# Block-causal attention with a ReGLU feed-forward on Trainium2: last-key scores placed behind the first score visit, and visits and products shifted, in the third tile

## The chip, the core and the metric

The kernel runs on one core of one Trainium2 chip, as one program. The metric is device time in microseconds (us). All engines work side by side: TensorE (PE) multiplies matrices, ScalarE (ACT) does exponentials and ReLU, VectorE (DVE) does elementwise arithmetic, GpSimd (POOL) issues the casting loads and does some elementwise work, SyncE (SP) issues the transposing transfers. Each engine executes its own list of instructions in the order in which the program wrote them; they meet at semaphores.

## The reference: what is computed

There are 8 batches, 8 heads, 576 positions, head size 64. Attention is causal by blocks of 64: a query sees the keys of its own block and of all earlier blocks. The attention output, joined over the heads to rows of 512, goes through a feed-forward with gate and value.

```python
scores = scale * np.matmul(q, k.transpose(0, 1, 3, 2))
scores = np.where(block_i >= block_j, scores, -1000000000.0)
attn = softmax(scores)                       # over the keys
x = np.matmul(attn, v)                       # to (8 * 576) x 512
out = (np.maximum(x @ w_gate, 0.0) * (x @ w_val)) @ w_out    # 512 -> 1536 -> 512
```

## The kernel before, in words

**Feed-forward tiles.** The rows of a batch are cut into 512 main rows and 64 tail rows. The feed-forward works on nine tiles of 512 rows: tile j (0 to 7) is the main rows of batch j, tile 8 collects the tail rows of all batches. One tile has 12 columns f of the hidden layer. For each f, four TensorE matmuls make the gate (over c = 0 to 3, a quarter of the 512 inputs each) and four make the value (L862, `ffn_gen`). ScalarE takes the ReLU of the gate (`relu`, L872), VectorE multiplies it with the value into `hT` (`hidden`, L882). From the third tile on (j >= 2) the product with `w_out` is done by a seven-product scheme (`seven_products`, L785), for which VectorE makes sums of `hT` (L744, one step after each ReLU from f = 4 on).

**Attention beside it.** The attention of batch b runs inside the feed-forward tile of batch b - 1, so in the third tile (j = 2) TensorE also works on the fourth batch (b = 3). It goes by rounds r = 4b + head pair, so here r = 12 to 15, each with these steps, named by a letter and r:

- s: the score visit (`visit`, L428, matmuls L451). It makes all scores of a head pair in four PSUM areas: the single buffer `one`, one `ffnp` buffer, and two `sc` buffers. From batch 3 on it also holds the 64 tail queries (`qTt`), which come right after the first pair of matmuls. ScalarE then takes the exponentials: one of `one`, one of `ffnp` (L463), one of the first `sc` buffer (L456).
- e: the exponential of the second `sc` buffer (L456), on ScalarE alone.
- c: zeroing of corners in the exponentials, on VectorE here (L1017), on POOL for r = 15.
- a, b: the product of the exponentials with v for the first and the second head (`products_with_v`, L586 and L600, 15 matmuls), then a normalisation on VectorE (L523, L525, L532).
- x: a transposing transfer of the result to `xT`, issued by SP (`to_xT_dma`, L635).

Two more steps belong to a batch: L3 is `last_keys(3)` (L469): four matmuls (L473) of the transposed last keys `kTt` with `qTt` into `one`, and an exponential into `attnL` (L480), which the products a and b read. B2 is the tail product of the third batch (`tail_av`, L539, matmuls L548).

**Where operands come from.** `d3` (at place 260.7) issues four transposing transfers from SP: `qTm`, `kTm` (L348), then `qTt`, `kTt` (`tails_by_dma`, L116 to L120). `l4`, `lv4` are POOL's loads of the fifth batch, `d4` its four transposes.

**Buffers.** PSUM holds two `sc` buffers, one `one` and three `ffnp` buffers (L47 to L55). Gates, values, the second head's part of a visit, and for r = 12, 13, 14 also both products a and b (`HOW`, L1367 to L1369) share the three `ffnp` buffers; a new user waits until the readers of the old one are done. `a15`, `b15` use `sc`.

**The order** is written out by hand. The dictionary `AT` gives every step a place. A place counts feed-forward matmuls: 144 to a tile, the third tile begins at 288. From the third tile on the first 96 places of a tile are its 96 gate and value matmuls. The loop emits the feed-forward up to a step's place and then the step, in order of places; steps with equal places keep the order of the dictionary:

```python
for n in sorted(acts, key=lambda n: AT[n]):
    at = int(place_of(AT[n]))
    ffn(at - place[0])
    place[0] = max(place[0], at)
    acts[n]()
```

Below, "place 28" means 28 matmuls into the third tile (316 in `AT`). Later tiles use one fixed pattern (`STEADY`, L1397): visits at places 2, 30, 58 and 86, then e 6, c 13, a 20 and b 24 places after their visit, the last products later.

Of the kernel before, what the change touches and what calls it, by code (L numbers as in the profile page):

```python
# [17 lines left out]
def kernel(  # L18
# [1003 lines left out]
    with tc.manual_schedule(engines={E.PE, E.DVE, E.Activation, E.Pool, E.SP}):  # L1022
# [82 lines left out]
        def mains_1(hp):  # L1105
# [209 lines left out]
            "E2": 283.05,  # L1315
            "L2": 286.35,
            "A2": 299.9,
            "s12": 316,
            "L3": 315.45,
            "l4": 319.56,  # L1320
            "e12": 324,
            "B2": 326.23,
            "lv4": 333.84,
            "c12": 331,
            "a12": 337,
            "b12": 341,
            "s13": 335,
            "e13": 343,
            "x12": 341.1,
            "d4": 356.12,  # L1330
            "c13": 350,
            "s14": 354,
            "e14": 362,
            "c14": 369,
            "a13": 356,
            "b13": 360,
            "x13": 360.1,
            "a14": 375,
            "b14": 379,
            "s15": 373,  # L1340
            "e15": 381,
            "x14": 379.1,
            "c15": 388,
            "a15": 400,
            "b15": 404,
# [210 lines left out]
```

## Time and profile before

| | us |
|---|---|
| median of 3 runs | 360.32 |
| fastest and slowest of them | 359.3, 362.04 |
| the profiled execution, its own time | 360.77 |
| its span, first to last instruction | 358.9 |
| TensorE busy in the span | 346.0 (96%) |
| VectorE busy | 208.3 (58%) |
| ScalarE busy | 180.5 (50%) |
| POOL busy | 141.1 (39%) |

The mean granted TensorE clock over the span was 0.997. The span is what the profile's views cover; the execution's own time is 1.87 us longer. The views name instructions by line, engine, operation and tile; `x4` means that four were merged into one row; the time given for a merged row is from the start of the first to the end of the last. The times of one matmul overlap with the next: a 128x512 matmul is shown as 379 ns, and four in a row start about 0.865 us before the row that follows them, or 0.216 us each. A number in square brackets is idle time of the engine before the row, and what ended it.

### The profile page before, as it was taken

The page shows a single profiled execution, that of the slowest core. Times are in us where ns is not written, and L with a number is a line of the kernel's source. Part 1 is how long each engine was busy: PE and PEld are TensorE (multiplying, and loading weights), DVE is VectorE, ACT ScalarE, POOL GpSimd, SP SyncE. Part 2 cuts the span into 40 slices and gives each one's busy share as a digit, 9 for nine tenths or more (in the row PEclk, how much of TensorE's full clock was granted, in tenths as well). Part 3 has the DMA queues.
Part 4 walks back from the last instruction along what each step waited for, and adds up shares of the span by engine and source line. Part 5 has one row for each costly group of instructions (what it writes and reads, how often), then busy time and mean ns, then how long its engine had stood idle before and what let it go on. Part 6 is the DMA issues. An engine that isn't in the chain of part 4 may idle for free.

```text
span 358.9 us, 8064 instructions
## 1 busy us (share of the span) xinstructions
PE 346.0 (96%) x3173; PEld 202.1 (56%) x3173; DVE 208.3 (58%) x522; ACT 180.5 (50%) x286; POOL 141.1 (39%) x183
## 2 busy tenths in 40 slices
PE   6899999999997999999999999999999999999994
PEld 2544455545543448555865576557755684485473
DVE  4663445678454775576637772667366745644661
ACT  5933766686335662556355545655475513322321
POOL 4647645599918602591049302950200020020002
PEclk9999999999999999999999999999999999999998
DMA  8999989999999993699549963998310030003004
GB/s 242 297 355 372 328 210 288 195 141 167 183 179 129 132 148 82 138 147 134 93 134 136 120 127 116 131 137 141 112 46 15 17 111 29 2 14 105 1 0 119
DMA packets 155495, 50.02 MB, mean 139 GB/s; under 512 B 134465, under 2 KB 151873, under 8 KB 155457
## 3 DMA queue, kind: packets, MB, share of 16 engines
q0 software_dynamic: 70480, 8.85, 48.4%
q1 hardware_dynamic: 76432, 31.47, 43.2%
q10 hardware_dynamic: 8544, 9.18, 7.8%
q8 instruction: 25, 0.41, 0.5%
q14 instruction: 14, 0.11, 0.1%
HBM read 37.75 MB, written 9.44 MB: 131 GB/s over the span
## 4 chain that ended last, share of the span: by engine, by line
PE 87%; DMA 6%; ACT 3%; POOL 1%; DVE 1%; issue 1%; SPq 0%; DVEq 0%; POOLq 0%
PE ffnp L862 50%; PE ffnp L785 13%; PE one L785 5%; PE ffnp L957 3%; PE sc L451 3%; PE ffnp L586 2%; PE one L451 2%; DMA xT<-xnat 2%; DMA stage<-in_moe_w_gate_dram 2%; PE one L586 1%; DMA stage<-in_k_dram 1%; PE one L862 1%; ACT attnT L456 1%; PE ffnp L548 1%; PE sc L586 1%; ACT attnT L463 1%
## 5 line engine op out<-in xcount | busy, mean ns | idle before, releaser
L882 DVE TENSOR_TENSOR hT<-gate_sb,ffnp 128x512 bf16<-128x512 bf16 x106 | 72.6, 685 | 73.7 <-PE ffnp L862 49.0
L862 PE MATMUL ffnp<-xT,wv 128*128 128x512 bf16 x376 | 102.0, 379 | 0.0
L872 ACT ACTIVATE gate_sb<-ffnp 128x512 bf16<-128x512 f32 x103 | 62.1, 605 | 78.3 <-PE ffnp L862 77.1
L862 PE MATMUL ffnp<-xT,wg 128*128 128x512 bf16 x364 | 100.3, 379 | 0.6 <-DVE xT L630 0.3
L862 PEld LDWEIGHTS <-wv 128*128 128x128 bf16 x432 | 39.8, 98 | 45.3 <-issue 3.6
L829 POOL TENSOR_TENSOR ob<-ob 128x512 f32<-128x512 f32 x7 | 8.8, 1263 | 142.6 <-ACT ob L826 142.6
L862 PEld LDWEIGHTS <-wg 128*128 128x128 bf16 x432 | 39.9, 98 | 43.2 <-issue 3.0
L456 ACT ACTIVATE attnT<-sc 128x1024 bf16<-128x1024 f32 x56 | 57.5, 1042 | 0.0
L785 PEld LDWEIGHTS <-stage 128*128 128x128 bf16 x420 | 40.3, 98 | 6.2
L744 DVE TENSOR_TENSOR stage<-hT 128x512 bf16<-128x512 bf16 (+2 forms) x84 | 38.5, 485 | 0.9
L586 PEld LDWEIGHTS <-attnT 128*128 128x128 bf16 x640 | 26.5, 98 | 13.4 <-issue 2.2
L785 PE MATMUL ffnp<-stage 128*128 128x256 bf16 x252 | 31.4, 273 | 0.0
L463 ACT ACTIVATE attnT<-one 128x512 bf16<-128x512 f32 (+1 forms) x28 | 15.0, 536 | 25.9 <-PE ffnp L451 25.8
L339 POOL DMA_DIRECT2D q_bf<-in_q_dram x20 | 18.0, 913 | 23.4 <-DVE hT L882 18.0
L339 POOL DMA_DIRECT2D v_bf<-in_v_dram x30 | 24.1, 842 | 0.9 <-PE sc L451 0.4
L957 PE MATMUL ffnp<-wo,hT 128*128 128x512 bf16 x96 | 23.6, 379 | 0.0
L451 PEld LDWEIGHTS <-kTm 64*128 64x128 bf16 x384 | 13.3, 94 | 14.1 <-issue 8.1
L451 PE MATMUL sc<-qTm,kTm 64*128 64x512 bf16 (+1 forms) x168 | 17.8, 305 | 0.0
L339 POOL DMA_DIRECT2D k_bf<-in_k_dram x20 | 17.7, 935 | 0.0
L785 PEld LDWEIGHTS <-hT 128*128 128x128 bf16 x168 | 16.4, 98 | 1.9
L837 DVE TENSOR_TENSOR ob<-ffnp,ob 128x512 f32<-128x512 f32 x7 | 4.8, 692 | 21.6 <-POOL ob L829 15.0
L826 ACT COPY ob<-ffnp 128x512 f32<-128x512 f32 x7 | 4.1, 586 | 21.9 <-PE ffnp L785 21.9
(143 smaller groups left out, 460.4 us busy)
## 6 DMA issues: line engine op xcount, KB each, us to landing
out_dram<-ob ACTq DMA_DIRECT2D x32, 256.0 KB, 2.4
stage<-in_moe_w_val_dram SPq DMA_DIRECT2D x6, 512.0 KB, 8.2
stage<-in_moe_w_gate_dram SPq DMA_DIRECT2D x6, 512.0 KB, 8.6
stage<-in_moe_w_out_dram SPq DMA_DIRECT2D x6, 512.0 KB, 10.6
q_bf<-in_q_dram POOLq DMA_DIRECT2D x20, 128.0 KB, 4.6
k_bf<-in_k_dram POOLq DMA_DIRECT2D x20, 128.0 KB, 5.8
v_bf<-in_v_dram POOLq DMA_DIRECT2D x20, 128.0 KB, 5.7
stage<-in_v_dram SPq DMA_DIRECT2D x19, 128.0 KB, 5.5
```

Of the source, the lines that this page charges most:

```text
L339: ins = nc.gpsimd.dma_start(dst, part_of)
L451: nc.tensor.matmul(o, kTm[b % 2][head_of(hh), c, hp, :], qT, start=True, stop=True)
L456: return lambda: nc.scalar.activation(at[:, :, lo : lo + 512], sc, AF.Exp, scale=scale)
L463: nc.scalar.activation(at[:, hh, 1024 : 1024 + w], third[hh][:, 0:w], AF.Exp, scale=scale)
L586: nc.tensor.matmul(av[:, p, :], at[:, col : col + 128], v_bf[b % 2][:, c, h, :], start=(p == 0), stop=(c == p), skip_group_check=True,)
L744: nc.vector.tensor_tensor(out=out.rearrange("p (c n) -> p c n", c=m), in0=a, in1=b, op=op)
L785: nc.tensor.matmul(to, sums.of(c)[which][:, 128 * p : 128 * p + 128], right, start=first, stop=(c == 5), skip_group_check=True,)
L829: nc.gpsimd.tensor_tensor(out=c22, in0=g, in1=c12, op=AX.add)
L862: nc.tensor.matmul(to, (wg, wv)[t][f // 4][:, c, 128 * (f % 4) : 128 * (f % 4) + 128], x[:, c], start=(c == 0), stop=(c == 3),)
L872: nc.scalar.activation(gate_sb, gate, AF.Relu)
L882: nc.vector.tensor_tensor(out=h, in0=gate_sb, in1=val, op=AX.mult)
L957: nc.tensor.matmul(op, hT[f][:, 128 * s : 128 * (s + 1)], wo[f // 4][:, f % 4, n0:n1], start=(f == 0), stop=(f == 11),)
```

## The change

Only places in `AT` change. In the third tile L3 moves from place 27, ahead of the visit s12, to place 45, behind s12 and ahead of s13. The steps of the rounds 12 to 14 move by up to 3.5 places:

| step | s12 | L3 | e12 | c12 | s13 | a12 | b12 | e13 | c13 | s14 | a13 | b13 | e14 | s15 | a14 | b14 |
|---|---|---|---|---|---|---|---|---|---|---|---|---|---|---|---|---|
| place before | 28 | 27 | 36 | 43 | 47 | 49 | 53 | 55 | 62 | 66 | 68 | 72 | 74 | 85 | 87 | 91 |
| place after | 30 | 45 | 38 | 45 | 48 | 52 | 56 | 56 | 63 | 66 | 70 | 74 | 74 | 85 | 88 | 92 |

x12, x13 and x14 follow their b as before. l4, B2, lv4, d4 and the steps of round 15 stay. No operation is added or removed, and no line of a function changes.

```diff
-            "s12": 316,
-            "L3": 315.45,
+            "s12": 318,
+            "L3": 333,
             "l4": 319.56,
-            "e12": 324,
+            "e12": 326,
             "B2": 326.23,
             "lv4": 333.84,
-            "c12": 331,
-            "a12": 337,
-            "b12": 341,
-            "s13": 335,
-            "e13": 343,
-            "x12": 341.1,
+            "c12": 333,
+            "a12": 340.5,
+            "b12": 344,
+            "s13": 336,
+            "e13": 344,
+            "x12": 344.1,
             "d4": 356.12,
-            "c13": 350,
+            "c13": 351,
             "s14": 354,
             "e14": 362,
             "c14": 369,
-            "a13": 356,
-            "b13": 360,
-            "x13": 360.1,
-            "a14": 375,
-            "b14": 379,
+            "a13": 358.5,
+            "b13": 362,
+            "x13": 362.1,
+            "a14": 376.5,
+            "b14": 380,
             "s15": 373,
             "e15": 381,
-            "x14": 379.1,
+            "x14": 380.1,
```

## The prediction

> **What bounds the kernel now.** I read the page first (busy time by engine), then the stages tile by tile, then TensorE's waits in the third tile, then TensorE's timeline there, then the transfers it waits for.
>
> ```profile
> PE 346.0 (96%) x3173; PEld 202.1 (56%) x3173; DVE 208.3 (58%) x522; ACT 180.5 (50%) x286; POOL 141.1 (39%) x183
> ```
>
> TensorE is busy for nearly the whole span and its clock is full, so only its idle time can be won. Where does that lie? The stages (columns: stretch, its length, then busy time of PE, PEld, DVE, ACT, POOL, clock, DMA share, GB/s) are the third, fourth and fifth tile:
>
> ```profile
> 101.80:144.58 42.78, 39.48 (x409) 23.78 (x408) 26.56 (x75) 20.85 (x33) 16.18 (x21) 1.00 1.35 134
> 144.58:182.00 37.42, 37.42 (x371) 23.23 (x369) 22.70 (x60) 20.23 (x32) 16.97 (x20) 1.00 1.37 136
> 182.00:219.40 37.40, 37.40 (x371) 23.24 (x369) 22.70 (x60) 20.23 (x32) 16.32 (x19) 1.00 1.52 126
> ```
>
> The tile that the change touches takes 42.78 us, its neighbours 37.4. Its only extra TensorE work is two tail products (A2, B2), 0.61 and 0.60 us from the timeline. So 42.78 - 37.41 - 1.21 = 4.16 us of it is waiting that the neighbours do not have. TensorE's waits in it, and one of its weight loads:
>
> ```profile
> PE one L473 <- DMA kTt<-k_bt: 2.4, 1, 2.4
> PE ffnp L586 <- ACT gate_sb L872: 0.3, 1, 0.3
> PE one L451 <- ACT attnL L480: 0.3, 1, 0.3
> PE ffnp L586 <- ACT attnT L463: 0.2, 1, 0.2
> PEld L586 <- DVE xtail L532: 1.0, 2, 0.5
> ```
>
> The first is L3, stopped by the transposed last keys. The third is s12, stopped by L3's exponential, because both use the one buffer `one`. The timeline around them:
>
> ```profile
> 107.86 0.81 PE L862 MATMUL ffnp<-xT,wg 128*128 128x512 bf16 x3
> 111.11 0.29 PE L473 MATMUL one<-qTt,kTt 128*128 128x64 bf16 x4 [2.43 <-DMA kTt<-k_bt]
> 111.23 0.38 PE L862 MATMUL ffnp<-xT,wg 128*128 128x512 bf16 x1
> 111.87 0.27 PE L451 MATMUL one<-qTm,kTm 64*128 64x256 bf16 x1 [0.26 <-ACT attnL L480]
> 112.64 1.04 PE L862 MATMUL ffnp<-xT,wv 128*128 128x512 bf16 x4
> ```
>
> And the four transposes of this batch, each with its issue on SP and its time from the start of the issue to landing:
>
> ```profile
> L348 SPq DMA_TRANSPOSE kTm<-k_bf x1: 4952/4952/4952, 102.1 to 102.1; - x1
> DMA to landing us min/median/max: 7.8/7.8/7.8
> L117 SPq DMA_TRANSPOSE qTt<-q_bt x1: 1181/1181/1181, 107.2 to 107.2; - x1
> DMA to landing us min/median/max: 3.2/3.2/3.2
> L118 SPq DMA_TRANSPOSE kTt<-k_bt x1: 1338/1338/1338, 108.5 to 108.5; - x1
> DMA to landing us min/median/max: 2.6/2.6/2.6
> ```
>
> With the issue times of SP's timeline (102.12, 107.18, 108.47) kTm lands at 109.9, qTt at 110.4, kTt at 111.06; qTm (97.29 + 9.5) at 106.8. The visit s12 needs all but kTt: kTm and qTm at its first matmul, qTt at its third.
>
> **The change part by part.** Matmuls of 512 columns count 0.216 us (four rows start 0.865 apart).
>
> *1. L3 leaves place 27.* TensorE is through place 27 at 107.86 + 3 x 0.216 = 108.51. Before, it idles to 111.11 (2.60), does L3 (0.12), one matmul (to 111.45), idles to 111.87 (0.42), and does s12 in 0.77, to 112.64. Two more matmuls bring it to 113.07 with 30 matmuls, L3 and s12 done.
>
> *2. s12 at place 30 now meets the transfers first.* TensorE gets there at 108.51 + 0.65 = 109.16. It waits for kTm until 109.92, does the first pair (0.11), waits for qTt until 110.4, and does the remaining 0.66: 111.05. L3, moved to place 45, still costs its 0.12, so the same work is done at an equivalent 111.17 instead of 113.07: **1.90 us** earlier. This rests on the transfers not moving: SP issues them from 97.29 on, long before the first changed instruction, and POOL's l4, which waits for the product of f = 2 (ended by 108.8), starts at 109.12 in both. Ends: if qTt came only with kTt at 111.06, 0.66 less; if it were ready, the whole 3.02 of idle time would go.
>
> *3. L3 at place 45.* kTt is there 3 us earlier. New is that s13 at place 48 follows it by three matmuls and needs `one` back. Before, s12 could start 0.76 after L3 did (111.11 to 111.87) with ScalarE free; now 0.12 + 0.65 = 0.77 lie between. But the ReLU of f = 5 (0.60) goes ahead of L3's exponential on ScalarE; it becomes ready about 0.05 before L3's matmuls start, so it can hold the exponential for at most 0.3. Queued behind that exponential are s13's. I take -0.10, ends 0 and -0.30. The products need its `attnL` at place 52, 1.5 us on: hidden.
>
> *4. a12 from two to four matmuls behind s13.* Before, s13 ended at 118.22 and a12 could have run at 118.66; it began at 119.02, when the second of s13's `ffnp` exponentials (118.38, 0.59 long) had freed a buffer. Four matmuls put it at 119.08 on that scale. **+0.36**, ends 0 and 0.36.
>
> *5. b12 four behind a12, as before.* It began at 120.51 instead of 120.34, when a12's normalisation on VectorE ended. The distance stays, so I take 0; +0.17 if it gets another buffer, -0.20 if VectorE's sums for f = 6 (0.67) now get ahead of that normalisation.
>
> *6. a13, b13 two places later; s14 stays at 66.* b13 began at 126.86 instead of 126.41, 0.45 lost: it needed the buffer of the gate of f = 8, whose ReLU stood on ScalarE behind three exponentials of s14 and ended at 126.81, 2.92 after s14 began. Now the gate of f = 9 comes between a13 and b13 and wants a buffer 0.77 + 4 x 0.216 + 0.45 + 2 x 0.216 = 2.51 after s14's start: the same wait under another name. I take 0. Ends: +0.45; -0.70 if b13 then needs the buffer of the value of f = 8, whose product on VectorE (0.69) follows that ReLU.
>
> *7. a14, b14 one place later* with s15 in place. b14 lost 0.16 behind a14's normalisation; VectorE is the crowded engine there and the sums for the seven products follow. **+0.08**, ends 0 and 0.16.
>
> *8. e12, e13, c12, c13, x12 to x14* move with them. e12 and e13 free `sc` buffers over 2 us before s13 and s14 need them (e13 lands ahead of the ReLU of f = 7, as before). The corners wait behind e on VectorE and end well ahead of the products. On SP x12 and x13 come later in place but earlier in time; d4 sits between them and its last transfer (issued 132.44, landing about 2.6 later, at 135.0) is needed by s16 at 145.11, or 2.2 earlier now: 7.8 us of cover. Cost nothing; if the cover were gone, s16 would pay as L3 did.
>
> Sum: 1.90 - 0.10 + 0.36 + 0 + 0 + 0.08 = **2.24 us**. Later tiles show no TensorE wait at all and hang on TensorE's own progress, so the gain should reach the end. Ceiling: 4.16, less the 1.12 that s12 still waits, is 3.04; the single ends upwards (1.90 + 0.36 + 0.17 + 0.45 + 0.16) give the same. Downwards, with qTt on time: 1.90 - 0.30 + 0 - 0.20 - 0.70 = 0.70.
>
> The profiled execution took 360.77 (span 358.9, 1.87 around it): 358.5 by the sum. It lies 0.45 above the median of the runs shown, 360.32, which becomes **358.1 us**.
>
> A rule against point 2: the Trainium skill, "DMA: Bandwidth & Descriptors", section "Queues, rings and completion order", says that transfers issued one after the other by SP do not have to complete in that order, since data descriptors carry no barrier. By it qTt could land with kTt or after it, and the sum would be 1.58 or less; the row has it 0.66 ahead, and no run here yet shows another order.
>
> **Rivals.**
>
> *A. The wait only changes its name.* s12 needs three of the four transfers, so it may stand nearly as long as L3 did. For it: kTm lands only 1.1 before kTt, all four share queue and transfer engines with POOL's loads. Against it: the landings above. With qTt at 111.06 the gain is 2.24 - 0.66 = 1.58: 358.7; with the low ends of points 3 to 6 as well it is 0.70 - 0.66 = 0.04: 360.3.
>
> *B. The tile becomes as clean as its neighbours.* For it: the new distances (a 22, b 26 behind the visit) are near those of the fourth tile (20 and 24), which shows no waits. Against it: there one product uses `one`, here both take `ffnp`, and visits are 18 apart, not 28. Gain 3.04: 357.3.
>
> *C. Slower: the three `ffnp` buffers become the bound.* Gates now fall between a and b of a round; each could wait for a ReLU behind exponentials (0.45, as b13 did) plus a VectorE product (0.69), 1.14. One such place leaves a gain; at three (rounds 12, 13, 14) the loss is 3.4 and the kernel ends at 360.3 + 3.4 - 2.2 = 361.5. It decides from two on (2.3 against 2.24). Against it: VectorE was idle for a third of this tile (26.56 of 42.78 busy), and the neighbours run the same mix of work without a wait.
>
> **How the numbers follow.** The forecast (gain 1.6 to 2.9) 0.62, A 0.18 (0 to 1.6), B 0.10, C 0.10, half of which still ends within 1% of before. The forecast's own range is 357.4 to 358.7. Together with A's larger part and B's it reaches from 357.0 to 360.0, which leaves out A's low end, C and the farthest of B: about 2 in 10. A measurement of this kernel can tell about 1%, 3.6 us, from no change; the ceiling of 3.04 lies under that, so faster by over 1% has 0.05, for waits I do not see; slower by over 1% has 0.05, half of C; within 1% has 0.90.
>
> **What would show it.** Point 1: no row in which L473 waits for kTt. Point 2: s12 starts at 109.9, its tail matmuls wait for qTt until 110.4, and the matmul after s12 starts near 111.1. Point 3: s13's first matmul waits at most 0.3 for L480. Point 4: a12's wait for L463 gone. Points 5 to 7: waits at b12, at the gate of f = 9 or at b13, and at b14, of 0.2, 0.45 and 0.1 at most. The third tile lasts 40.5 instead of 42.8, and the fourth still 37.4. Wrong would be: qTt landing with kTt, a wait of the size of a VectorE product in two rounds, or any later tile that takes more than 37.4.

## The result, and the profile after

The changed kernel takes 358.51 us against 361.26 us before (medians of 8 runs each), a ratio of 0.9927 with a 95% interval of 0.9899 to 0.9955. Two later sets, on two chips, gave 0.995 (0.9927 to 0.9973) and 0.9958 (0.9931 to 0.9984). So it is faster, by 1.5 to 2.6 us, 0.4 to 0.7%, taken from the ratios. One of the eight runs of the changed kernel, at 364.69 us, fell into a slower state of the chip and does not count in the ratio. The profiled execution took 358.44 with a span of 356.7; before, 360.77 and 358.9: 2.2 us less in the span.

The third and the fourth tile in the stages of the profile after (same columns as before, with the length of the stretch first):

```profile
101.95:142.58 40.63, 38.79 (x409) 24.04 (x408) 26.28 (x75) 20.64 (x33) 16.15 (x21) 1.00 1.39 140
142.58:179.99 37.41, 37.41 (x371) 23.23 (x369) 22.71 (x60) 20.23 (x32) 17.01 (x20) 1.00 1.39 136
```

The third tile went from 42.78 to 40.63, its neighbour is as it was. Two TensorE waits are left in it, out of four:

```profile
PE one L451 <- DMA kTm<-k_bf: 1.6, 1, 1.6
PE ffnp L862 <- ACT gate_sb L872: 0.3, 1, 0.3
```

L3 no longer waits; s12 now does. TensorE's timeline after, at the same place:

```profile
108.59 0.59 PE L862 MATMUL ffnp<-xT,wv 128*128 128x512 bf16 x2
110.74 0.28 PE L451 MATMUL one<-qTm,kTm 64*128 64x256 bf16 x1 [1.55 <-DMA kTm<-k_bf]
...
111.67 0.60 PE L862 MATMUL ffnp<-xT,wv 128*128 128x512 bf16 x2
...
115.52 0.28 PE L473 MATMUL one<-qTt,kTt 128*128 128x64 bf16 x4
...
116.42 0.27 PE L451 MATMUL one<-qTm,kTm 64*128 64x256 bf16 x1
```

TensorE is through place 30 at 108.59 + 2 x 0.216 = 109.02, as forecast (109.16), but s12 begins at 110.74 and ends at 111.67, where 109.9 and 111.05 were forecast. Why, the transfers say. SP's issues after, and below them each transfer's time from issue to landing, in the order kTm, qTt, kTt:

```profile
101.83 5.03 SPq L348 DMA_TRANSPOSE kTm<-k_bf  x1
106.96 1.19 SPq L117 DMA_TRANSPOSE qTt<-q_bt  x1
108.26 2.49 SPq L118 DMA_TRANSPOSE kTt<-k_bt  x1
```

```profile
DMA to landing us min/median/max: 8.9/8.9/8.9
DMA to landing us min/median/max: 4.0/4.0/4.0
DMA to landing us min/median/max: 6.7/6.7/6.7
```

They were issued when they were before, within 0.3 us, but kTm landed at 110.7 instead of 109.9, qTt at 111.0 instead of 110.4, and kTt, the last keys, at 115.0 instead of 111.06. Had kTt landed then under the old order, L3 would have stood until 115.0.

Where the 2.0 us up to the start of the fourth tile (144.58 before, 142.58 after) came from, each a difference of gaps in TensorE's two timelines:

| part | forecast, us | measured, us |
|---|---|---|
| up to place 27 (108.51, now 108.38) | 0 | +0.13 |
| place 27 to 30 matmuls, L3 and s12 done (4.56, now 111.67 - 108.38 + 0.12 = 3.41) | +1.90 | +1.15 |
| s13 behind L3 (gap 0.09, now 0.14) | -0.10 | -0.05 |
| a12 (gap 0.36, now none) | +0.36 | +0.36 |
| b12 (gap 0.17, now none) | 0 | +0.17 |
| b13 (gap 0.45), now the gate of f = 9 (0.45) | 0 | 0 |
| b14 (gap 0.16, now none) | +0.08 | +0.16 |
| sum | 2.24 | 1.92 |

The 0.08 between 1.92 and 2.0 is not placed. Another 0.2 of the 2.2 us in the span lies behind the fourth tile, which ends 2.0 earlier (179.99 against 182.00). The 0.13 ahead of place 27 is no effect of the change: before, a gap of 0.25 in the tile's first four matmuls ended when a piece of xT landed, and here there is none.

### The profile page after: what moved, and what is told of

Read it like the earlier page. It is cut to its first block, busy times and chain, and to the rows that moved or that the text cites. A ratio compares the mean times of both kernels' runs of the same rounds, so it can differ in the third digit from the quotient of the medians.

```text
span 356.7 us, 8063 instructions
## 1 busy us (share of the span) xinstructions
PE 346.3 (97%) x3173; PEld 203.3 (57%) x3173; DVE 207.5 (58%) x522; ACT 180.5 (51%) x286; POOL 141.1 (40%) x183
## 4 chain that ended last, share of the span: by engine, by line
PE 91%; ACT 3%; DMA 2%; DVE 2%; issue 0%; POOL 0%; POOLq 0%; DVEq 0%
PE ffnp L862 49%; PE ffnp L785 13%; PE one L785 5%; PE ffnp L957 5%; PE sc L451 3%; DMA kTm<-k_bf 2%; PE one L451 2%; PE ffnp L586 2%; PE one L586 2%; PE one L862 1%; PE sc L586 1%; PE one L1008 1%; ACT attnT L456 1%; PE ffnp L270 1%; PE ffnp L548 1%; PE sc L401 1%
```

## The experiments

Theory M: the gain is the wait of L3 for kTt, taken off TensorE's path and limited by the landing of kTm and qTt, plus the small waits at the products. Rival D: the larger distances of the products are what counts, and s12 simply waits in L3's place. The first set asks which, and what makes the transposes land when they do.

### The changed kernel again

> The changed kernel once more, to see which of its numbers repeat. Theory M (the gain is the wait of the last-key scores for kTt, taken off TensorE's path, limited by when kTm and qTt land): 2.2 to 2.7 us faster than before, s12 held 1.1 to 1.9 in all by kTm and qTt, and kTt landing at any time up to 115 without effect. Theory D (what counts is the larger distance of the products from their visits, 0.36 at a12, 0.17 at b12, 0.16 at b14 in the first profile): the same time; this run does not tell them apart.

Measured: 359.54 us against 360.98, ratio 0.995 (0.9927 to 0.9973), so 1.8 us faster, a little under the 2.2 to 2.7 expected. TensorE's waits up to the fourth tile in this execution:

```profile
PE one L451 <- DMA qTt<-q_bt: 1.5, 1, 1.5
PE ffnp L862 <- DMA xT<-xnat: 0.7, 1, 0.7
PE ffnp L862 <- ACT gate_sb L872: 0.3, 1, 0.3
```

This time the tile's first matmuls also waited, for the last piece of xT, and s12's first pair ran at 110.48, just behind kTm's landing at 110.4, but its tail matmuls stood until 112.27 for qTt (issued 107.68, landed 4.6 later, at 112.3). The waits for ScalarE and at the products repeat; the landing of the transposes does not. The landing of qTt is a moment that varies by 2 us from one execution to the next, and what TensorE loses to it depends on when it gets there: a wait for xT at the tile's start takes away from a wait for kTm or qTt later.

### L3 alone, and all but L3

```diff
 e1_only_l3, against the kernel before
-            "L3": 315.45,
+            "L3": 331.5,
 e2_l3_first, against the changed kernel
-            "L3": 333,
+            "L3": 315.45,
```

> The kernel before with one step moved: L3 from place 27 to place 43, behind s12, which stays at 28. Theory M: TensorE is at s12 at about 108.7, waits for kTm and qTt until 110.4 to 111.0 and is done at 111.05 to 111.7, where before it was at 112.64 with L3 (0.12) done too: 0.85 to 1.5 us faster than before; the waits of 0.36 at a12, 0.45 at b13 and about 0.16 at b12 and b14 stay as they were. Theory D: under 0.4 us faster, since s12 only waits in L3's place.

> The changed kernel with one step put back: L3 at place 27, ahead of s12, which stays at 30; visits and products keep their new places. Theory M: TensorE waits at L3 for kTt as before (2.4 us if it lands at 111.06, more if later), s12's wait for the buffer of L3 (0.42) is gone because three matmuls lie between, and the waits at a12, b12 and b14 are gone: 0.7 to 1.2 us faster than before, 1.2 to 1.8 slower than the changed kernel. Theory D: as fast as the changed kernel to within 0.5 us.

Measured on one chip with the run above: e1 359.18 us, ratio 0.9956 (0.9936 to 0.9976), 1.6 us faster than before; e2 360.07 us, ratio 0.9986 (0.9956 to 1.0017), 0.5 us, not clear of no change. In e1's waits (first fence) L3 and s12 are gone and the products' are still there; in e2 (second fence) it is the other way round:

```profile
PE ffnp L862 <- DMA xT<-xnat: 1.6, 1, 1.6
...
PE ffnp L586 <- ACT gate_sb L872: 0.3, 1, 0.3
PE ffnp L586 <- ACT attnT L463: 0.2, 1, 0.2
```

```profile
PE one L473 <- DMA kTt<-k_bt: 1.8, 1, 1.8
PE ffnp L862 <- DMA xT<-xnat: 1.6, 1, 1.6
PE ffnp L862 <- ACT gate_sb L872: 0.3, 1, 0.3
```

D asked for under 0.4 from e1, which refutes it. For e2 it asked for the time of the changed kernel to within 0.5 us; e2 is slower by 1.3 us by the ratios, as M has it (1.2 to 1.8), but only by 0.5 by the medians (360.07 against 359.54), so e2 alone would not decide. Moving L3 carries most of the gain, as M has it, though e1's 1.6 is a little over M's 0.85 to 1.5.

### The fifth batch's loads later

```diff
-            "l4": 319.56,
+            "l4": 340.2,
-            "lv4": 333.84,
+            "lv4": 340.3,
```

> The changed kernel with POOL's loads of the fifth batch (q and k, and v behind them) moved from places 31 and 45 to place 52, so that they start some 9 us later and do not run beside the last transposes of the fourth batch. If those loads hold the transposes up: kTt lands by 111.5 instead of 114.96, kTm and qTt land at most 0.3 earlier since they land about when the loads begin, and the time stays within 0.5 us of the changed kernel. If the landing of the transposes varies by itself or is held by something else: kTt lands as late as 113 to 115 again. The loads have time: the fifth batch's first visit is 30 us away, and its transposes then end some 5 us later; if they came too late, the visit at the start of the fourth tile would wait.

Measured: 366.52 us, ratio 1.0161 (1.0129 to 1.0193), 7 us slower than the changed kernel on the same chip (359.54). Neither case of the expectation came as written. qTt landed at 107.81 + 4.4 = 112.2, no earlier than with the loads beside it, so in this execution the loads do not set its landing; kTt's issue took 1.36 instead of 2.49, and it landed at 112.8, between the 111.5 and the 113 of the two cases. And the loads did come too late. SP's issues in the third tile show how:

```profile
127.62 4.75 SPq L348 DMA_TRANSPOSE qTm<-q_bf  x1
132.60 8.19 SPq L348 DMA_TRANSPOSE kTm<-k_bf  x1
...
143.52 2.53 SPq L635 DMA_TRANSPOSE xT<-xnat  x2
```

x13 and x14, whose data were ready, stand behind the fifth batch's transposes in SP's list and are issued at 143.5, when the fourth tile wants them; its first matmuls then wait 1.86, 1.43 and 2.26 us for xT, 5.55 in all. Behind these waits the granted clock of TensorE was 0.50 from 150 to 155 us and 0.88 from 155 to 160 (in the changed kernel 1.00 in both), and a row of four matmuls at 155.25 shows 1.51 us instead of 1.03: that adds to the loss. The price of late loads was paid by another transfer, through the order of SP's list.

### Further placings: s12 later, s14 later

```diff
 e3_s12_36, against the changed kernel
-            "s12": 318,
+            "s12": 324,
-            "e12": 326,
+            "e12": 330.5,
 e4_s14_68, against the changed kernel
-            "s14": 354,
+            "s14": 356,
-            "e14": 362,
+            "e14": 364,
```

> The changed kernel with s12 moved on from place 30 to 36 and e12 from 38 to 42; L3, the products and everything else as in the changed kernel. Theory T (what s12 waits for is a point in time, the landing of qTt at 110.4 to 112.3, and any feed-forward matmul put ahead of it fills that wait): six matmuls, 1.3 us, go into a wait of 1.3 to 1.9 us, so 1.0 to 1.5 us faster than the changed kernel, some 3 us faster than before, and s12's first matmul waits for 0.6 us at most. Theory U (the wait only moves on, to a12 at place 52, whose exponentials come later by as much): within 0.4 us of the changed kernel, with a new wait of TensorE at s13 or a12.

> The changed kernel with s14 moved from place 66 to 68, behind the ReLU of f = 8, and e14 from 74 to 76. If the 0.45 us that TensorE waits at the gate of f = 9 come from that ReLU standing behind three exponentials on ScalarE: the wait is gone and the kernel is 0.45 us faster than the changed one. If the buffer is held by something else, VectorE's normalisation of a13 for instance: a wait of 0.2 us or more stays there or at b13.

Measured, on one chip: e3 358.44 us against 361.93, ratio 0.9906 (0.9876 to 0.9937), the best of the placings; e4 359.77 us, ratio 0.9949 (0.992 to 0.9979), like the changed kernel, which did not run on this chip. In e3's profile kTm landed at 112.04, the latest of all profiles, s12 still waited 1.22 for it, and yet the fourth tile began at 142.6, no later than in the changed kernel's first profile with kTm at 110.7: from place 27 on it took 33.7 us (108.88 to 142.59) against 34.2 (108.38 to 142.58). The six matmuls ahead of s12 filled a part of the wait, and no wait came up at a12. That speaks for theory T and against U, though T's limit of 0.6 us for s12's first matmul did not hold. In e4 the wait at the gate of f = 9 is gone and one of 0.17 at b13 came up, so it was the ReLU behind the exponentials; the 0.28 won is too small for these rounds, and in this profile a wait of 0.50 for VectorE (L842) at the start of the fourth tile took it back.

### The stores away from the transposes

What stretches the transposes? Before, ScalarE issues three 256 KB stores of the second tile's output just ahead of them:

```profile
93.87 0.35 ACTq L648 DMA_DIRECT2D out_dram<-ob  x1
98.24 0.34 ACTq L648 DMA_DIRECT2D out_dram<-ob  x1
101.65 0.34 ACTq L648 DMA_DIRECT2D out_dram<-ob  x1
```

The changed kernel issues them 0.13 later. The transfer queues between 104 and 108 us in the profile after (q1 holds SP's transposes, q10 the stores; packets, MB, share of 16 engines):

```profile
q1 hardware_dynamic: 2194, 0.55, 76.7%
q10 hardware_dynamic: 238, 0.43, 42.5%
```

So the stores were held back, first to f = 6, 8, 10 of the third tile, at the same place in ScalarE's list as a ReLU. `SEVEN` is 2, the third tile; the second edit keeps the second tile (j = 1) from issuing them itself:

```diff
-                        if j > SEVEN and f == 1:
-                            store.pop()()
+                        if f in {SEVEN: (6, 8, 10)}.get(j, (1,) if j > SEVEN else ()):
+                            store.pop(0)()
...
-                if store:
+                if store and j != 1:
                     store.pop()()
```

> The changed kernel with three 256 KB stores of the second tile's output, issued by ScalarE at about 94, 98 and 102 us, held back to f = 6, 8 and 10 of the third tile. Theory S (the stores share the transfer engines with the transposes: between 104 and 108 they took 45% of them beside the transposes' 72%): xT, kTm and qTt land 1 to 2 us earlier, TensorE no longer waits for xT at the start of the third tile and for 0.5 us at most at s12, 1 to 2 us faster than the changed kernel. Theory P (the transposes go at a pace of their own, 4 to 5 us of issue for each large one): qTt lands between 110.4 and 112.3 as before, and the time is within 0.4 us.

> The three edits of the last runs in one kernel: s12 at 36 with e12 at 42, s14 at 68 with e14 at 76, and the three stores held back. Theories T and S: s12 waits for nothing, the third tile takes 39 us or less, and the kernel is 2 to 3 us faster than the changed one, 4 to 5 faster than before. Theories U and P: 0.5 us faster than the changed kernel, from s14 alone.

Measured: e8 359.6 us, ratio 0.9937 (0.9901 to 0.9973), with single runs from 356.75 to 362.04; e9, all three edits, 358.68 us, ratio 0.9895 (0.9846 to 0.9944), 3.8 us faster than before where 4 to 5 were expected. e9's profile is of a run of 362.34 us and is not read. In time e8 does not bear out theory S: by the ratios of two sets it is 0.5 us faster than the changed kernel, not 1 to 2. In its profile, of one of its fastest runs, S holds, and the landings come earlier by more than the 1 to 2 us that it gave. SP's issues are shorter and the landings, kTm first, then qTt, are

```profile
101.59 2.22 SPq L348 DMA_TRANSPOSE kTm<-k_bf  x1
103.92 1.31 SPq L117 DMA_TRANSPOSE qTt<-q_bt  x1
```

```profile
DMA to landing us min/median/max: 4.3/4.3/4.3
DMA to landing us min/median/max: 2.5/2.5/2.5
```

that is 105.9 and 106.4 instead of 110.7 and 111.0, no wait for a transfer is left in the tile, and the span is 354.9. But the stores now lie beside the fifth batch's transposes, whose kTm takes 10.2 to land instead of 4.3 in the changed kernel; POOL's loads lie beside it too. What its slower runs wait for no profile here shows.

So the last set puts the stores between the two batches' transposes, at f = 3, 4 and 5: in e10 with the changed order, in e11 with the order of before, in e12 with s14 at 68. The edit is that of e8 with (3, 4, 5) in place of (6, 8, 10).

> The changed kernel once more, as the measure for the three runs beside it on the same chip: 1.8 to 2.7 us faster than before.

> The changed kernel with the three stores of the second tile held back to f = 3, 4 and 5 of the third tile (about 108, 112 and 115 us) instead of 6, 8 and 10, so that they pass between the fourth batch's transposes and the fifth's, beside POOL's loads. Theory S (stores beside large transposes stretch them, and every later transpose waits behind them on SP): qTt lands at 106 to 107 in place of 110.4 to 112.3, s12 waits for no transfer, and the fifth batch's kTm lands within about 5 us of its issue as without the stores, so the time is 1.2 to 2 us below the changed kernel and its spread small. Theory R (what is taken from one batch's transposes is paid by the next transfers, now POOL's loads): the fifth batch's transposes come later and the start of the fourth tile waits for xT; the time is that of the changed kernel, or above.

> The kernel before, with only the three stores held back to f = 3, 4 and 5 of the third tile; L3 stays ahead of s12. Theory S: kTt lands at about 108.3, when TensorE reaches L3 at 108.5, so L3 waits for 0.5 us at most; s12's wait for L3's buffer (0.42) and the waits at a12, b12, b13 and b14 (1.1 together) stay; 2 to 2.8 us faster than before without any change to the order of L3. If the transposes were not what L3 waited for in the first place, or do not follow the stores: L3 waits 2 us or more as before, and the time is that of before.

> The kernel with the stores at f = 3, 4 and 5, and s14 at place 68 and e14 at 76 as in an earlier run. With the transfers out of the way the 0.45 us at the gate of f = 9 are the largest wait left in the third tile; s14 behind the ReLU of f = 8 takes about 0.28 of it away net (a wait of 0.17 at b13 came up in its place): 0.2 to 0.4 us faster than with the stores alone, or no difference that these rounds can tell.

| one chip, before 361.08 | us | ratio (95% interval) | span of the profile |
|---|---|---|---|
| c1, the changed kernel | 359.23 | 0.9958 (0.9931 to 0.9984) | 356.6 |
| e11, order of before, stores moved | 358.16 | 0.9921 (0.989 to 0.9951) | 356.0 |
| e10, changed order, stores moved | 357.32 | 0.9897 (0.9855 to 0.9938) | 355.3 |
| e12, as e10 with s14 at 68 | 357.07 | 0.9886 (0.9847 to 0.9926) | 355.3 |

The transfer queues between 104 and 108 us in e10 (first fence, q1 alone; q10 has no row), and TensorE at L3 and s12 in e11 (second fence):

```profile
q1 hardware_dynamic: 2068, 0.51, 73.2%
```

```profile
107.71 0.81 PE L862 MATMUL ffnp<-xT,wg 128*128 128x512 bf16 x3
108.36 0.28 PE L473 MATMUL one<-qTt,kTt 128*128 128x64 bf16 x4
108.48 0.38 PE L862 MATMUL ffnp<-xT,wg 128*128 128x512 bf16 x1
109.11 0.27 PE L451 MATMUL one<-qTm,kTm 64*128 64x256 bf16 x1 [0.26 <-ACT attnL L480]
```

L3 in its old place does not wait at all; what stays in e11 are exactly the small waits of before: 0.41 at s12, 0.35 at a12, 0.17 at b12, 0.45 at b13, 0.17 at b14. e10 differs from e11 by the change alone: from place 27 to the fourth tile 32.4 us (108.34 to 140.76) against 33.5 (108.36 to 141.82), 1.0 us, which is 0.41 + 0.35 + 0.17 + 0.17 less 0.05 at s13. Theory S is borne out for the time, but not in all: e10's fifth-batch transposes took 11.0 (qTm) and 10.3 (kTm) to land, not the 5 expected, and it cost nothing, since the visit that needs them is late enough. No store lies beside these; POOL's loads do (the packets of their queue q0 make 84.1% of the 16 engines' time while kTm is under way, and none of them falls there in the changed kernel, where kTm took 4.3). So stores are not the only transfers that go with a long transpose, and e8's 10.2 cannot be put down to them alone. c1 came out at 1.5 us by its ratio, under the 1.8 to 2.7 expected. e10's six runs lie between 357.1 and 357.56, those of the kernel before in this set between 358.62 and 363.87. e10 and e12 beat both kernels; between the two the rounds tell no difference.

## Why the prediction was right, point by point

- **Points 1 and 2** (L3 off the path, s12 meets the transfers: 1.90). The mechanism is shown: e1 wins 1.6 with this step alone, and e2, without it, loses most of it by the ratios. The size was off: 1.15 in the profile. The step that failed is "this rests on the transfers not moving". In the profile after, their issue moved by 0.3 us at most, but their landing is no fixed time: in the nine profiles with the stores in their old place qTt was issued between 106.4 and 108.4 and landed between 110.4 and 112.3. The forecast took one execution's landing for a constant. What it lacked is the main cause of the late landing, three stores on the transfer engines at that time; in the four profiles of e8, e10, e11 and e12 qTt lands at 106.4 to 106.9.
- **Point 3** (-0.10): -0.05. kTt came at 115.0 and L3 was at 115.52; the 3 us by which kTt was to be early were 0.5 in this execution.
- **Point 4** (+0.36): +0.36, confirmed by e11 against e10.
- **Point 5** (0): +0.17, its upper end; b12 waits in no profile read here of a kernel with the new places, and in the profile after it starts at 119.39, ahead of the end of a12's normalisation (119.51), so it no longer needs a12's buffer first.
- **Point 6** (0, the wait under another name): as said, 0.45 at the gate of f = 9, and e4 shows that it is the ReLU behind s14's exponentials.
- **Point 7** (+0.08): +0.16, its upper end.
- **Point 8** (nothing): right for this change; e7 shows the price when SP's cover is gone, 7 us, and that x13 and x14 pay it first, not s16 as I wrote. s16's own qTt landed at 145.3 there, some 1 us after TensorE would have come to it without these waits.
- **Rivals.** A was partly true: of 3.02 us of idle time ahead of and at s12, 1.88 remained (1.72, and 0.16 at the tail matmuls). What speaks for it names a shared queue; the views have SP's transposes on q1 and POOL's loads on q0, so the 16 transfer engines are what they share. B came about, but for the 0.45 at the gate of f = 9, only when the stores were moved. C did not occur: one gate between a and b waits, and only for the ReLU.
- **The rule** that transfers issued by SP one after the other need not land in that order: in no profile here did a batch's four transposes land in another order. kTt landed 0.5 to 4.0 us after qTt; what varied was when.

That the sum of 2.24 was met (2.2 in the span) is in part luck: a loss of 0.75 at s12 was made up by 0.30 more than forecast at s13, b12 and b14, by a tile start that in this execution had no wait for xT (0.13), and by 0.3 that the forecast has no term for. Over the three sets the gain is 1.5 to 2.6, so the last lies just under the forecast's 1.6 to 2.9. The time, 358.51, lies in the range of 357.4 to 358.7, which was counted from a median of 360.32; against this set's own 361.26 the gain was larger than forecast, and in the two later sets the changed kernel took 359.54 and 359.23, above the range.

## What to carry to other kernels

When a step waits for a transfer, ask first what else is on the transfer engines at that time: moving three stores was worth 2.9 us with no change of order (e11), more than the reordering beside it (c1, 1.5 by its ratio), which moved TensorE's work around a late transfer. A landing read from one execution is a sample; a forecast that stands on it needs its spread, and the work put ahead of the waiting step (e3) is what makes an order insensitive to it. Before a transfer or a load is moved, look who stands behind it in the issuing engine's list: in e7 two ready transposes paid for late loads.

## What the runs showed of the hardware that was not expected

- A large transposing transfer takes longer when other transfers run beside it (shares are packet time; queues overlap, so one can pass 100%). kTm from issue to landing, for the fourth and the fifth batch in the 13 profiles read here:

  | beside kTm (share of the 16 engines until it landed) | transfers | us to landing | issue on SP, us |
  |---|---|---|---|
  | nothing but SP's transposes | 8 | 4.3 to 4.4 | 1.8 to 2.8 |
  | POOL's loads, under 10% | 3 | 4.5 to 6.4 | 3.0 |
  | the stores, 23 to 31% | 9 | 6.9 to 9.1 | 4.0 to 5.6 |
  | POOL's loads, 60% and more (in e7 also a little of a store, 6%) | 5 | 9.4 to 11.5 | 5.1 to 8.2 |
  | stores 20% and POOL's loads 30% (e8) | 1 | 10.2 | 5.4 |

  For the stores e11 shows which is cause and which effect, since there only they were moved; for the loads no run does. Nor does a run show what they share inside the transfer engines or the memory behind them.
- The single runs lie 5.3 us apart before (23 runs), 3.5 in e11 (twelve; eleven of them within 1.0), 2.1 in e12 (six) and 0.5 in e10 (six), the last three with the stores at f = 3, 4 and 5. That the stretching makes the spread is not shown.
- A transfer issued last can be late by itself: kTt took 2.6 us before and 6.7 after, with POOL's loads starting 0.7 us after its issue in both. In the three profiles where it took over 5 us (after, c0, e3) its issue took 2.3 to 2.6 us instead of 1.2 to 1.4, and it lay beside POOL's loads; with the loads moved away (e7) it took 3.7. What made its issue long in only some of the executions stays open.
